# Two queues for one weight load: wq of problem A in two column ranges on the SP and ACT queues, x behind it on the ACT queue

## The chip, the cores and the metric

The kernel runs on one core of one Trainium2 chip. The metric is the device time of one execution in microseconds (us). Executions of one kernel agree within about 0.3%, so medians and ratios are quoted, and a trace is one execution and not the median one.

## The reference, cut to what matters

Two independent problems, A and B, of the same shape: one decode step of attention over the last 4096 positions of a key and value cache, 32 query heads on 16 key heads, batch 2, head size 128, model size 576.

```python
q = x @ wq                                   # (2, 576) @ (576, 4096), bf16
k = k_cache[:, :, -4096:, :]; v = v_cache[:, :, -4096:, :]
# cut: reshapes, and the repeat of each key and value head for its two query heads
scores = einsum("bhqd,bhkd->bhqk", q, k) * 128 ** -0.5
o = einsum("bhqk,bhkd->bhqd", softmax(scores), v)
out = o @ wo                                 # (2, 4096) @ (4096, 576)
# for A and for B; the outputs stand side by side
```

The bytes are almost all cache: 32 slabs of 4 MB (16 of K, 16 of V), beside 4.7 MB for each wq and each wo. x is 2.3 KB per problem.

## The kernel before

The cache slabs go through a ring of four SBUF slots (`NSLOT = 4`, 32 KB per partition and slot). At the start the two wq matrices lie in slots 0 to 2 of that ring. The first K slab goes to slot 3 at once; the second goes to slot 0 and must wait until q of A is done with wq of A. This ring of slots is one thing; where the text below speaks of a queue's ring, or of x's own ring, it means the row of packets that one queue (SP or ACT) has waiting on one DMA engine. A packet is one contiguous row of a copy, or the 4-byte write to a semaphore that ends a copy.

```python
def f_x(e):                                   # four copies of 2 rows of 1,152 bytes
    for P in range(NPROB):
        for h in range(2):
            last = e.dma_start(x8[4*P+2*h : 4*P+2*h+2, :], probs[P][0][:, 0, :]).then_inc(x_sem, 16)
    return last
x_dma = dma_op("act", x_sem, 2 * NPROB, f_x, [], "x")          # ACT queue, waits for nothing

for P in range(NPROB):                        # each wq: 128 rows of 36,864 bytes, SP queue
    def f_wq(e, P=P):
        src = probs[P][3].rearrange("a b -> (a b)").rearrange("(p f) -> p f", p=128)
        return e.dma_start(ringf[:, P*QW:(P+1)*QW], src).then_inc(wq_sem[P], 16)
    wq_dma[P] = dma_op("sp", wq_sem[P], 1, f_wq, [], "wq%d" % P)
# ... cut: x -> VectorE mask (xs8) -> TensorE transposes (xT) -> ACT copy (op_xev) ...
q_done[P] = pe(f_q, [wq_dma[P], op_xev], "q%d" % P)            # 36 matmuls for each P
# ... cut ...
stream = []                                   # order of the loads in the SP queue: K0 K1 K2 K3 V0 K4 V1 ...
for t in range(NSLAB + LAG):
    if t < NSLAB:
        stream.append(("K", t))
    if t >= LAG:
        i = t - LAG
        if i % 4 == 0 and i > 0:
            stream.append(("M", i // 4 - 1))  # a wo load
        stream.append(("V", i))
# ... cut ...
first_deps = {0: [q_done[0]], 1: [q_done[0], q_done[1]], 2: [q_done[1]], 3: []}   # by ring slot
```

Of the kernel before, what the change touches and what calls it, by code (L numbers as in the profile page):

```python
# [62 lines left out]
def build_kernel(nc, probs, out):  # L63
# [3 lines left out]
    NPROB = len(probs)  # L67
# [19 lines left out]
    UW = HD // 2  # L87
    NU = (2 * D) // 128
    QW = NU * UW
# [3 lines left out]
    with es:  # L93
# [50 lines left out]
        ringf = ring[:].rearrange("p r f -> p (r f)")  # L144
# [9 lines left out]
        sem = lambda name: es.enter_context(nc.semaphore(name))  # L154
# [3 lines left out]
        lastv_sem = [sem("lastv%d" % k) for k in range(2)]  # L158
        w_cuts = [0, 4, 7, 8]
        lastw_sem = [sem("lastw%d" % k) for k in range(2)]  # L160
        wq_sem = [sem("wq%d" % P) for P in range(NPROB)]
        wo_sem = [sem("wo%d" % r) for r in range(2)]
        x_sem = sem("xload")
        out_sem = sem("outdone")
# [4 lines left out]
        def dma_op(eng, sem_h, n_dmas, fn, deps, tag):  # L169
            op = S.add(eng, fn, deps, tag)  # L170
            dma_count[sem_h] = dma_count.get(sem_h, 0) + 16 * n_dmas
            op.dma = (sem_h, dma_count[sem_h])
            return op

        def f_x(e):
# [2 lines left out]
                for h in range(2):  # L178
                    last = e.dma_start(x8[4 * P + 2 * h:4 * P + 2 * h + 2, :], probs[P][0][:, 0, :]).then_inc(x_sem, 16)
            return last  # L180
        x_dma = dma_op("act", x_sem, 2 * NPROB, f_x, [], "x")

        wq_dma = {}
        for P in range(NPROB):
            def f_wq(e, P=P):
                src = probs[P][3].rearrange("a b -> (a b)").rearrange("(p f) -> p f", p=128)
                return e.dma_start(ringf[:, P * QW:(P + 1) * QW], src).then_inc(wq_sem[P], 16)
            wq_dma[P] = dma_op("sp", wq_sem[P], 1, f_wq, [], "wq%d" % P)

        pool = lambda fn, deps, tag: S.add("pool", fn, deps, tag)  # L190
        dve = lambda fn, deps, tag: S.add("dve", fn, deps, tag)
        act = lambda fn, deps, tag: S.add("act", fn, deps, tag)
        pe = lambda fn, deps, tag: S.add("pe", fn, deps, tag)
# [5 lines left out]
        p_ident_b = pool(lambda e: e.affine_select(ident_b[:], ones_b[:], [[-1, 128]], ALU.is_equal, 0.0,  # L199
                                                   base=0, channel_multiplier=1), [p_ones_b], "ident_b")  # L200
        p_zxU = pool(lambda e: e.memset(pTf[:, 0:XW].bitcast(FP32), 0.0), [], "zero_xU")

        def f_sel(e):
            last = None
            for p4 in range(4):
                b32, par = p4 // 2, p4 % 2
                last = e.affine_select(sel[:, p4, :].rearrange("d (a p) -> d a p", a=4),
                                       ones_b[:, :].rearrange("d (a p) -> d a p", a=4),
                                       [[0, 4], [-2, 32]], ALU.is_equal, 0.0, base=-(64 * b32 + par), channel_multiplier=1)
            return last  # L210
# [35 lines left out]
        def mm_held(e, o, wt, mv_, first, tile=None):  # L246
            size, at = tile or ((128, 128), (0, 0))
            return e.add_instruction(mybir.InstMatmult(  # L248
                name=nc.get_next_instruction_name(), engine=mybir.EngineType.PE,
                ins=[e.lower_ap(mv_), e.lower_ap(wt, for_matmul_weights=True)], outs=[e.lower_ap(o)],  # L250
                start_tensor_calc=first, stop_tensor_calc=True, bass_skip_group_check=True, ldweights=False,
                tile_size=size, tile_position=at))
# [14 lines left out]
        op_xev = act(f_xev, [op_xT, p_zxU], "xev")  # L267
        tb_consumer[n_] = op_xev

        q_done = {}  # L270
        QB = [OTB[0:32, :], PJT[0][0:32, :], PJT[1][0:32, :], STT[1][0:32, 512:1024]]
        for P in range(NPROB):
            def f_q(e, P=P):
                for u in range(NU):
                    for c in range(4):
                        wt, mv_ = xU[:, P, u, :], wqv[P][:, u, c * 512:(c + 1) * 512]
                        first = P == 0 and u == 0
                        if c == 0:
                            last = e.matmul(QB[c], wt, mv_, start=first, stop=True, skip_group_check=True)  # L279
                        else:  # L280
                            last = mm_held(e, QB[c], wt, mv_, first, ((128, 32), (0, 0)))
                return last
            q_done[P] = pe(f_q, [wq_dma[P], op_xev], "q%d" % P)
        q_ev = [act(lambda e, k=k: e.activation(qrow[32 * k:32 * k + 32, :], QB[k], ACTF.Copy), [q_done[1]], "qe%d" % k)
                for k in range(4)]

# [460 lines left out]
        for op in order:  # L747
            have = seen[op.eng]
            need = {}
            for d in op.deps:  # L750
# [3 lines left out]
                k = id(s_h)  # L754
# [30 lines left out]
def bass_concat_heads__sliding_block_cached__sliding_block_cached__decode_kernel(  # L785
    nc, A_x, A_k_cache, A_v_cache, A_wq, A_wo, B_x, B_k_cache, B_v_cache, B_wq, B_wo, out,
):
    build_kernel(nc, [(A_x, A_k_cache, A_v_cache, A_wq, A_wo), (B_x, B_k_cache, B_v_cache, B_wq, B_wo)], out)
# [28 lines left out]
```

## Time and profile before

| | before |
|---|---|
| median of 5 runs | 363.09 us (363.01 to 364.5) |
| bytes read | 153.1 MB; the SP queue's packets fill 98.5% of the span of the 16 engines |
| mean rate | 423 GB/s |
| x landed / first q matmul | 13.05 / 15.65 us |
| second K slab issued / its first packet | 25.75 / 34.08 us |

The first view is the page's row of 40 equal slices (9.07 us each): the busy share of the 16 DMA engines in tenths, and what they moved.

```profile
DMA  8999999999999999999999999999999999999995
GB/s 326 447 431 416 448 417 441 426 430 437 430 435 408 455 408 426 454 419 444 420 435 426 434 434 414 440 441 412 452 414 442 426 441 420 438 423 441 407 422 220
```

Only the first slice (start) and the last (tail) are below 400 GB/s. The engines never stand idle in between, so this kernel's time is its start, plus its bytes, plus its tail. Work on TensorE, VectorE or ACT matters only where it delays the release of a ring slot so long that the SP queue runs out of loads.

The next view is the sum by stretches of time; its columns are the stretch, its length, the busy time of each engine with the count of instructions, the granted TensorE clock, the DMA share, and GB/s.

```profile
core 0: us, PE busy (x) PEld busy (x) DVE busy (x) ACT busy (x) POOL busy (x), PEclk, DMA share, GB/s
34.00:40.00 6.00, 1.19 (x9) 0.58 (x9) 4.78 (x2) 2.99 (x10) 1.04 (x4) 0.76 1.01 437
40.00:100.00 60.00, 45.13 (x184) 9.37 (x110) 46.28 (x19) 4.98 (x8) 3.68 (x14) 0.85 1.01 434
```

The same six us from 34 to 40 in 40 slices of 0.15 us (busy share in tenths; slices so narrow show zeros even in a busy stretch):

```profile
DMA  5999550059995500599955005999550059995500
```

Then the start of the chain of waits (start, length, what), which shows that x, and not wq, lets q begin. wq of A, issued at 0.80, landed 13.8 us later, at 14.6.

```profile
1.94 11.11 DMA tmp<-in_B_x_dram
13.08 1.35 DVE pR L217
14.48 0.71 PE tb L258 x9
15.21 0.30 ACT pT L265 x2
15.65 0.59 PE ot L279
```

Last, the SP queue's own timeline around the second and third K slabs (start, length of the issue, queue, line, what):

```profile
25.75 0.54 SPq L377 DMA_DIRECT2D ring<-in_A_k_cache_dram  x1
33.52 1.18 SPq L377 DMA_DIRECT2D ring<-in_A_k_cache_dram  x2
```

The second K slab was issued at 25.75, when q of A was done. The packet records that lie in the trace (one for each packet: start, duration, size, queue) show the engines turning to it only at 34.08, when the first slab's rows had all been started.

### The profile page before, as it was taken

The page shows a single profiled execution, that of the slowest core. Times are in us where ns is not written, and L with a number is a line of the kernel's source. Part 1 is how long each engine was busy: PE and PEld are TensorE (multiplying, and loading weights), DVE is VectorE, ACT ScalarE, POOL GpSimd, SP SyncE. Part 2 cuts the span into 40 slices and gives each one's busy share as a digit, 9 for nine tenths or more (in the row PEclk, how much of TensorE's full clock was granted, in tenths as well). Part 3 has the DMA queues.
Part 4 walks back from the last instruction along what each step waited for, and adds up shares of the span by engine and source line. Part 5 has one row for each costly group of instructions (what it writes and reads, how often), then busy time and mean ns, then how long its engine had stood idle before and what let it go on. Part 6 is the DMA issues. An engine that isn't in the chain of part 4 may idle for free.

```text
span 362.7 us, 2629 instructions
## 1 busy us (share of the span) xinstructions
PE 237.2 (65%) x1295; PEld 58.2 (16%) x935; DVE 211.9 (58%) x141; ACT 46.2 (13%) x80; POOL 22.1 (6%) x83
## 2 busy tenths in 40 slices
PE   0397687767665868471696666562586677667666
PEld 0010111112111212020131211110112121112222
DVE  0201898495949392924919492942917658585522
ACT  1002100140041001300014001400005000500500
POOL 3100101100010001000010001000010001000000
PEclk9999698969898888986798989889789687889986
DMA  8999999999999999999999999999999999999995
GB/s 326 447 431 416 448 417 441 426 430 437 430 435 408 455 408 426 454 419 444 420 435 426 434 434 414 440 441 412 452 414 442 426 441 420 438 423 441 407 422 220
DMA packets 6228, 153.28 MB, mean 423 GB/s; under 512 B 700, under 2 KB 840, under 8 KB 1224
## 3 DMA queue, kind: packets, MB, share of 16 engines
q1 hardware_dynamic: 6196, 153.10, 98.5%
q8 instruction: 9, 0.15, 0.2%
q10 hardware_dynamic: 20, 0.01, 0.0%
q14 instruction: 3, 0.02, 0.0%
HBM read 153.10 MB, written 0.00 MB: 422 GB/s over the span
## 4 chain that ended last, share of the span: by engine, by line
DMA 48%; DVE 25%; PE 16%; issue 8%; ACT 1%; SPq 0%; POOL 0%; ACTq 0%
DMA ring<-in_B_k_cache_dram 25%; DVE xt L432 15%; DMA ring<-in_A_k_cache_dram 13%; DMA ring<-in_B_v_cache_dram 8%; PE st L248 5%; PE st L458 4%; DMA tmp<-in_B_x_dram 3%; PE pj L248 3%; DVE oR L564 2%; DVE mx L466 2%; DVE pT L505 2%; DVE tmp L557 2%; ACT pR L496 1%; PE ot L279 1%; PE pj L635 1%
## 5 line engine op out<-in xcount | busy, mean ns | idle before, releaser
L458 PE MATMUL st<-xt,zq 128*128 128x512 bf16 x256 | 122.6, 479 | 89.9 <-DVE xt L432 89.8
L432 DVE STREAM_TRANSPOSE xt<-ring 128x4096 f32<-128x4096 f32 x32 | 141.6, 4429 | 36.3 <-DMA ring<-in_A_k_cache_dram 20.8
L248 PE MATMUL st<-xt,zq 128*128 128x512 bf16 x256 | 121.2, 473 | 0.0
L496 ACT ACTIVATE pR<-st,bias 128x512 bf16<-128x512 f32 x32 | 40.0, 1415 | 217.7 <-DVE bias L489 217.7
L458 PEld LDWEIGHTS st<-xt,zq 128*128 128x128 bf16 x256 | 29.0, 113 | 212.7 <-DVE xt L432 106.7
L535 PE MATMUL ot<-ring,pT 128*32 128x512 bf16 x512 | 32.5, 395 | 6.9 <-DMA ring<-in_B_v_cache_dram 4.4
L489 DVE SCALAR_TENSOR_TENSOR bias<-vmask,tb,offm 128x4 f32<-128x4 f32 x8 | 1.8, 223 | 36.1 <-PE tb L486 36.1
L519 DVE TENSOR_REDUCE ssum<-tb 128x2 f32<-128x8 f32 x8 | 1.3, 162 | 36.0 <-PE tb L516 36.0
L505 DVE STREAM_TRANSPOSE pT<-pR 128x2048 bf16<-128x2048 bf16 x8 | 18.4, 2304 | 0.7 <-ACT pR L496 0.7
L424 POOL TENSOR_TENSOR zq<-qs,bmask 128x64 bf16<-128x64 bf16 x32 | 8.6, 292 | 165.7 <-PE st L248 143.8
L557 DVE SCALAR_TENSOR_TENSOR tmp<-ot,rsb,dmask 128x512 f32<-128x512 f32 x16 | 11.5, 719 | 8.5 <-PE ot L535 8.4
L535 PEld LDWEIGHTS ot<-ring,pT 128*32 128x32 bf16 x512 | 12.6, 99 | 22.0 <-DMA ring<-in_B_v_cache_dram 8.9
L564 DVE TENSOR_REDUCE oR<-tmp 128x128 f32<-128x512 f32 x15 | 15.6, 1042 | 0.5
L248 PE MATMUL pj<-ring,pT 128*32 128x512 bf16 x36 | 11.9, 417 | 0.0
L248 PE MATMUL pj<-wob,oM 128*2 128x288 bf16 x48 | 11.9, 286 | 0.0
L616 PE MATMUL pj<-wob,oM 128*2 128x288 bf16 x48 | 11.9, 286 | 0.0
L258 PE MATMUL tb<-ident_b,pR 8*128 8x8 bf16 x9 | 0.7, 198 | 14.5 <-DVE pR L217 14.5
L466 DVE TENSOR_REDUCE mx<-st 128x2 f32<-128x1024 f32 x8 | 9.7, 1214 | 0.1
L496 ACT ACTIVATION_READ_ACCUMULATOR pR<-st,bias 128x1 f32 x32 | 8.9, 278 | 0.0
L217 DVE TENSOR_TENSOR pR<-tmp,hmask 8x1152 bf16<-8x1152 bf16 x1 | 1.3, 1345 | 11.5 <-DMA tmp<-in_B_x_dram 11.5
L279 PE MATMUL ot<-ring,pT 128*32 128x512 bf16 x18 | 7.5, 419 | 0.5 <-ACT pT L265 0.5
L248 PE MATMUL st<-ring,pT 128*32 128x512 bf16 x18 | 7.3, 407 | 0.0
(69 smaller groups left out, 71.4 us busy)
## 6 DMA issues: line engine op xcount, KB each, us to landing
ring<-in_A_k_cache_dram SPq DMA_DIRECT2D x8, 4096.0 KB, 24.9
ring<-in_A_v_cache_dram SPq DMA_DIRECT2D x8, 4096.0 KB, 29.9
ring<-in_B_k_cache_dram SPq DMA_DIRECT2D x8, 4096.0 KB, 28.6
ring<-in_B_v_cache_dram SPq DMA_DIRECT2D x7, 4096.0 KB, 29.9
ring<-in_A_wq_dram SPq DMA_DIRECT2D x1, 4608.0 KB, 13.8
ring<-in_B_wq_dram SPq DMA_DIRECT2D x1, 4608.0 KB, 24.2
wob<-in_A_wo_dram SPq DMA_DIRECT2D x2, 2304.0 KB, 29.8
wob<-in_B_wo_dram SPq DMA_DIRECT2D x1, 2304.0 KB, 27.4
```

Source lines behind the costliest of these rows:

```text
L248: return e.add_instruction(mybir.InstMatmult(name=nc.get_next_instruction_name(), engine=mybir.EngineType.PE, ins=[e.lower_ap(mv_), e.lowe ...
L279: last = e.matmul(QB[c], wt, mv_, start=first, stop=True, skip_group_check=True)
L424: last = e.tensor_tensor(dst, src, msk, ALU.mult)
L432: Xop[(t, jh)] = dve(lambda e: e.transpose(xt[:, jh, :].bitcast(FP32).rearrange("p (kp x kt) -> p x kp kt", kp=2, kt=2), ring[:, r, jh * H ...
L458: last = e.matmul(ob, wt, mv_, start=first, stop=True, skip_group_check=True)
L466: ch[(G, "max")] = dve(lambda e: e.tensor_reduce(mx[:], st[:, :].rearrange("p (x t) -> p t x", t=2), AX.X, ALU.max), [Sop[(2 * G + 1, 1)]] ...
L496: last = e.activation(pR[:].rearrange("p (x k) -> p k x", k=4)[:, kv, :], st[:, :].rearrange("p (x t) -> p t x", t=2)[:, kv % 2, :], ACTF.Exp,
L505: pT_op[G] = dve(lambda e: e.transpose(pT[:, v, :].rearrange("p (w j q) -> p j w q", w=4, q=8), pR[:].rearrange("p (j w q) -> p j w q", w= ...
L535: last = e.matmul(OTB[32 * c:32 * c + 32, :], pT[:, v, base + 32 * c:base + 32 * c + 32], ring[:, r, jj * 128:(jj + 4) * 128], start=rd == ...
L557: evac_op[i] = dve(lambda e: e.scalar_tensor_tensor(tv, o, rsb[:, v, b:b + 1], dm, ALU.mult, ALU.mult), deps, "ev%d" % i)
L564: ch[(G, "red%d" % b)] = dve(lambda e: e.tensor_reduce(oR[:, b, :], tmp[:].rearrange("p (j d) -> p d j", j=4), AX.X, ALU.add), [evac_op[i] ...
L616: last = e.matmul(PJ[h], oM[:, j, :], mv_, start=start and j == 0, stop=True, skip_group_check=True)
```

## The change

The intent, as far as the edit tells it, is to have wq of A arrive by two queues at the same time, and to keep the small x copies from getting in the way of it: they now follow on the ACT queue, and also wait for a Pool memset.

```diff
-        wq_sem = [sem("wq%d" % P) for P in range(NPROB)]
+        wq_sem = [sem("wq%d" % P) for P in range(NPROB + 1)]
...
-        x_dma = dma_op("act", x_sem, 2 * NPROB, f_x, [], "x")
...
-            def f_wq(e, P=P):
-                src = probs[P][3].rearrange("a b -> (a b)").rearrange("(p f) -> p f", p=128)
-                return e.dma_start(ringf[:, P * QW:(P + 1) * QW], src).then_inc(wq_sem[P], 16)
-            wq_dma[P] = dma_op("sp", wq_sem[P], 1, f_wq, [], "wq%d" % P)
+            src = probs[P][3].rearrange("a b -> (a b)").rearrange("(p f) -> p f", p=128)
+            cuts = [("sp", 0, 5 * UW), ("act", 5 * UW, QW)] if P == 0 else [("sp", 0, QW)]
+            wq_dma[P] = []
+            for k, (q, c0, c1) in enumerate(cuts):
+                def f_wq(e, P=P, src=src, c0=c0, c1=c1, k=k):
+                    return e.dma_start(ringf[:, P * QW + c0:P * QW + c1], src[:, c0:c1]).then_inc(wq_sem[2 * k + P], 16)
+                wq_dma[P].append(dma_op(q, wq_sem[2 * k + P], 1, f_wq, [], "wq%d_%d" % (P, k)))
...
         p_zxU = pool(lambda e: e.memset(pTf[:, 0:XW].bitcast(FP32), 0.0), [], "zero_xU")
+        x_dma = dma_op("act", x_sem, 2 * NPROB, f_x, [p_zxU], "x")
...
-            q_done[P] = pe(f_q, [wq_dma[P], op_xev], "q%d" % P)
+            q_done[P] = pe(f_q, wq_dma[P] + [op_xev], "q%d" % P)
```

UW is 2,048 columns and QW is 9 UW, so each of the 128 rows of 36,864 bytes becomes one of 20,480 bytes on SP and one of 16,384 bytes on ACT.

## The prediction

> What bounds the kernel. The page puts the DMA share at 9 tenths in 38 of 40 slices, mean 423 GB/s for 153.28 MB; the first slice (326 GB/s) is the start, the last (220) the tail. The SP queue carries 98.5%. The trace's packet records show every engine starting a 36,864-byte wq row each 1.36 us and a 32 KB cache row each 1.21 us, without a gap from 2.1 to about 354 us. So the time is start + bytes + tail; compute matters only where it lets the SP queue run dry.
>
> What moves. Before, four x copies (1,152-byte rows, two engines) sit on the ACT queue from 0.8 us and land at 13.05 (the chain of waits: 11.11 us). The Trainium skill, "DMA: Bandwidth & Descriptors", section "Queues, rings and completion order", says that an engine round-robins between queue rows packet by packet. The packet records agree: each x copy is a data and a semaphore packet per engine, and after the first copy those start 1.36 to 1.45 us apart, one per wq row. x, not wq, lets q start: wq A lands at 14.6, and x + 1.35 (VectorE) + 0.7 (TensorE) + 0.3 (ACT) gives 15.5; the first q matmul is at 15.65.
>
> After, the same bytes of wq A run on two rings: a 20 KB and a 16 KB packet, together one old row, so wq A still lands at about 14.5. The same page, section "Issuing engines are not separate DMA queues", says both issuers share the same engines; only under 0.5 us of issue time could be gained. But x now stands in the ACT ring behind eight 16 KB packets, is reached at about 14 us, and then its eight packets alternate with the eight rows of wq B. I estimate from the 1.36 us row that x lands at 24 to 25.2 us. The wait for the Pool memset (done by 2.2 us) costs nothing.
>
> What follows. q of A starts at 26.5 to 27.8 instead of 15.65, takes about 10 us as before, and is done at 36.6 to 37.9 instead of 25.7. The second K slab waits for it (ring slot 0). Before, it was issued 7 to 8 us early: the last row of the first slab started at 33.2, the next at 34.4. Now it is late; with 1.3 us from issue to first packet (0.80 to 2.12 at the start) its first row starts at 37.9 to 39.2: a hole of 3.5 to 4.8 us in the DMA, plus up to 0.8 for refilling (the first row at the start cost 2.13, not 1.36). The third slab waits for q of B, done at 44.5 to 46, while the second arrives until about 48: no second hole. Scores start 10 to 11 us later, but slots were released 8 to 20 us ahead of need (fifth K slab 54.4 against about 73), so this is absorbed; the tightest, the sixth (issued 83.3, needed about 92), keeps some 3 us. All of the hole is on the critical path; the tail is unchanged.
>
> Sum: 363.1 + 4.3 = 367.4 us (+1.2%). Range 364.6 to 369.8. Faster by over 2%: 0.02; within: 0.90; slower: 0.08.
>
> To check: VectorE's idle time for x near 22 to 23 us instead of 11.5; first q matmul near 27; low bandwidth at 35 to 39 us; DMA otherwise full; tail as before.
>
> What would make it wrong: x's packets not alternating with wq B (x lands near 15: time unchanged); a later slot release falling behind, opening a second hole (over 370); two rings filling the start better (0.5 us faster).

## The result, and the profile after

| | before | after |
|---|---|---|
| median of 5 runs | 363.09 us | 369.11 us (367.95 to 369.92) |
| ratio | | 1.0157, 95% interval 1.0133 to 1.0181 |
| x landed / first q matmul | 13.05 / 15.65 | 25.16 / 27.75 us |
| second K slab issued / first packet | 25.75 / 34.08 | 37.16 / 38.51 us |

Ratios here are the mean time of one kernel's runs over the mean of the other's runs of the same rounds, so they are not quite the ratio of the medians. The change costs 1.6%, 5.7 us. The same slices of the page, now 9.18 us each:

```profile
DMA  8996899999999999999999999999999999999996
GB/s 314 458 425 289 343 411 445 439 418 450 407 453 409 450 432 420 434 441 414 447 411 441 432 432 425 437 425 446 414 443 413 447 428 432 427 432 432 416 415 253
```

Two slices, the fourth and the fifth, fell to 289 and 343 GB/s; everything after them is as full as before. The stretches of the same cuts:

```profile
34.00:40.00 6.00, 6.00 (x30) 0.68 (x7) 4.72 (x2) 0.00 (x0) 0.00 (x0) 1.00 0.28 87
40.00:100.00 60.00, 42.93 (x195) 9.02 (x113) 37.42 (x14) 8.46 (x18) 4.35 (x16) 0.89 1.01 433
```

A finer cut of 34 to 40 us, into 40 slices of 0.15 us, shows where the engines stood (busy share in tenths). Slices so narrow show a few zeros in a busy stretch too, because the view does not spread a packet over all of its time: what counts is the unbroken run of 30 zeros, 34.0 to 38.5 us, in which no packet starts. The rows started before it (the last at 33.60) end between 34.0 and 34.8 us, and each engine's next row starts between 38.5 and 39.2: each stood idle for some 4.4 to 4.8 us.

```profile
DMA  0000000000000000000000000000009909900000
```

From 34 to 40 us the engines moved 87 GB/s instead of 437, while TensorE was busy for all 6.00 us. The chain of waits and the SP queue say why:

```profile
3.44 21.72 DMA tmp<-in_B_x_dram
25.18 1.36 DVE pR L220
26.59 0.71 PE tb L261 x9
27.32 0.30 ACT pT L268 x2
27.75 0.59 PE ot L282
37.16 0.54 SPq L380 DMA_DIRECT2D ring<-in_A_k_cache_dram  x1
```

x took 21.72 us to land where it took 11.11. The steps behind it have the same lengths as before (1.36, 0.71, 0.30), so q of A starts 12.1 us later. It takes 0.7 us less than in before's trace (experiment 9), and the second K slab is issued at 37.16, 11.4 us later. The slack was 34.08 - 25.75 - 1.34 = 7.0 us (issue to first packet took 1.3 us in later runs where the queue was empty), so 4.4 us are left as the hole: 38.51 against 34.08.

The packet records show x's way through the ring. These are the starts of x's packets on one of the two engines that carry it (each of the four copies is one data packet of 1,152 bytes and one semaphore packet), in us:

| | copy 1 | copy 2 | copy 3 | copy 4 |
|---|---|---|---|---|
| before: data, semaphore | 1.72, 2.19 | 5.31, 6.72 | 8.08, 9.49 | 10.86, 12.26 |
| after: data, semaphore | 14.81, 16.22 | 17.58, 18.99 | 20.36, 21.76 | 23.13, 24.54 |

Two things delay it in after. Its first packet comes 13.1 us later, because eight rows of wq and their semaphore write stand ahead of it in its own ring, and each of those has its turn only after a packet of the other ring. The semaphore write counts: on this engine it came at 13.44, the first row of wq of B ran from 13.45 to 14.81, and only then was it x's turn. Then its eight packets take 9.7 us more, one for each 1.36 us row of wq of B. That two rows of x use two engines is what the Trainium skill, "DMA: Bandwidth & Descriptors", section "Why a DMA increments its semaphore by 16 and not by 1", says of a copy with two rows; the records agree with eight data packets for four copies, that is two for each.

A caution on the two traces. The profiled run of before had a time of 363.97, 0.9 above its median, and its last load packet ended 3.4 us before the end of the span; in after that tail was 2.6 us. So the spans (362.7 and 367.1) differ by 4.4 us only, but the last load packets (359.29 and 364.54) by 5.25. What makes the tail differ is said under "The sum over the runs".

### The profile page after: what moved, and what is told of

Read it like the earlier page. It is cut to its first block, busy times and chain, and to the rows that moved or that the text cites. A ratio compares the mean times of both kernels' runs of the same rounds, so it can differ in the third digit from the quotient of the medians. Undisturbed runs are those within 1.5% of the kernel's fastest.

```text
span 367.1 us, 2627 instructions
## 1 busy us (share of the span) xinstructions
PE 235.5 (64%) x1294; PEld 57.5 (16%) x935; DVE 211.4 (58%) x141; ACT 46.4 (13%) x80; POOL 22.2 (6%) x83
## 4 chain that ended last, share of the span: by engine, by line
DMA 35%; DVE 32%; PE 21%; issue 8%; ACT 2%; POOL 1%; ACTq 0%; SPq 0%; DVEq 0%; POOLq 0%
DVE xt L435 20%; DMA ring<-in_B_k_cache_dram 16%; DMA ring<-in_B_v_cache_dram 8%; PE st L251 7%; DMA tmp<-in_B_x_dram 6%; PE st L461 6%; DMA wob<-in_B_wo_dram 5%; PE pj L251 4%; DVE oR L567 3%; DVE pT L508 2%; DVE mx L469 2%; DVE tmp L560 2%; PE pj L619 2%; ACT pR L499 1%; PE ot L282 1%
## 5 line engine op out<-in xcount | busy, mean ns | idle before, releaser
L538 PE MATMUL ot<-ring,pT 128*32 128x512 bf16 x512 | 33.6, 405 | 4.5 <-DVE ssum L522 2.5
L220 DVE TENSOR_TENSOR pR<-tmp,hmask 8x1152 bf16<-8x1152 bf16 x1 | 1.3, 1347 | 23.6 <-DMA tmp<-in_B_x_dram 23.6
L282 PE MATMUL ot<-ring,pT 128*32 128x512 bf16 x18 | 7.3, 405 | 0.5 <-ACT pT L268 0.5
## 6 DMA issues: line engine op xcount, KB each, us to landing
wob<-in_A_wo_dram SPq DMA_DIRECT2D x2, 2304.0 KB, 27.8
ring<-in_A_wq_dram SPq DMA_DIRECT2D x1, 2560.0 KB, 13.8
```

Of the source, the lines that this page charges most:

```text
L282: last = e.matmul(QB[c], wt, mv_, start=first, stop=True, skip_group_check=True)
L538: last = e.matmul(OTB[32 * c:32 * c + 32, :], pT[:, v, base + 32 * c:base + 32 * c + 32], ring[:, r, jj * 128:(jj + 4) * 128], start=rd == ...
```

## The experiments

Eleven kernels ran; all gave correct results. The theory: x lands late because of its place in the ACT ring and because rings take turns packet by packet; that makes q of A late, the second K slab late, and the DMA engines idle; this hole is the whole loss. The rivals: (R1) cutting wq over two rings costs in itself; (R2) scores that start 10 us late push later slot releases; (R3) rings share by bytes and not by turns; (R4) the wait for the Pool memset is a part of it. Each set of runs has its own runs of before on the same chip; their medians were 363.36 (experiments 1, 2, 5 and 6), 363.18 (3, 4, 7 and the first run of 8) and 363.37 (the second run of 8, 9 and 10).

### 1. Late x without the split (against R1)

```diff
 # in the kernel before
-        x_dma = dma_op("act", x_sem, 2 * NPROB, f_x, [], "x")
...
             wq_dma[P] = dma_op("sp", wq_sem[P], 1, f_wq, [], "wq%d" % P)
+        x_dma = dma_op("sp", x_sem, 2 * NPROB, f_x, [], "x")
```

> The kernel before, wq of A in one piece on SP; the x copies are moved to the SP queue behind wq of B. Theory (late x alone makes the loss): x lands at 24 to 25.5 us, the first q matmul at about 27.5, the second K slab's first packet at 38 to 38.5, bandwidth falls to nothing from about 35 to 38, time 368.3 to 369.5, as after. Rival (cutting wq of A over two rings costs in itself): nothing is cut here, so the loss should be clearly smaller than after's 6 us.

Measured: 369.49 us, ratio 1.0171 (1.0156 to 1.0186). Its timeline has x consumed at 25.49 and the second K slab issued at 38.34:

```profile
25.49 1.34 DVE L217 TENSOR_TENSOR pR<-tmp,hmask 8x1152 bf16<-8x1152 bf16 x1 [23.93 <-DMA tmp<-in_B_x_dram]
38.34 0.53 SPq L377 DMA_DIRECT2D ring<-in_A_k_cache_dram  x1
```

Nothing is cut here, nothing runs on two rings, and the loss is the same. A late x is enough. (The first packet of the second slab came at 39.67, past the 38.5 that I had expected: q of A began at 28.06 and not at 27.5, and it took 10.25 us; on its length see experiment 9.)

### 2. Fill the hole (against R2)

```diff
 # in the kernel after
             if t < NSLAB:
                 stream.append(("K", t))
+            if t == 0:
+                stream.append(("M", 0))
...
-                if i % 4 == 0 and i > 0:
+                if i % 4 == 0 and i > 4:
```

> The kernel after with one edit: the first wo load (2.36 MB, no dependency) moves in the SP queue from among the V slabs to just behind the first K slab. Theory (all of the loss is the DMA engines standing idle before the second K slab): x still lands at about 25, q of A still starts at 27.75, but the wo load takes 5.4 us of engine time where the hole was, so the time returns to 362.7 to 363.7. Rival (scores that start 10 us late push later slot releases, or the split itself costs): x and q are as late as in after, so the time stays near 369.

Measured: 363.93 us, ratio to before 1.0009 (0.9992 to 1.0026). x and q are as late as in after (first q matmul 27.69, second K slab issued at 38.07), but 34 to 40 us are full:

```profile
34.00:40.00 6.00, 6.00 (x29) 0.68 (x7) 4.97 (x2) 0.00 (x0) 0.00 (x0) 1.00 1.02 425
```

Against after's 87 GB/s in the same stretch this is the decisive line: with the lateness untouched and only the idle engine time used for bytes that had to be moved anyway, the loss is gone within what this run resolves (its median lies 0.2 us above the range I had written). The 10 us by which the scores start late cost nothing that can be measured.

### 3. Control: the early wo load in the kernel before

The same edit as in 2, made in before.

> Control for the filling run: the kernel before with the first wo load just behind the first K slab. Theory: the DMA engines are busy there anyway, the same bytes in another order: 362.8 to 363.6. If the early wo load were a gain by itself, it would be below 361.

Measured: 363.42 us, ratio 1.0004 (0.9984 to 1.0023). The early wo load is no gain by itself; in 2 it only filled the hole.

### 4. The split with x behind wq of A on SP (R1 again)

```diff
 # in the kernel after
-        x_dma = dma_op("act", x_sem, 2 * NPROB, f_x, [p_zxU], "x")
...
                 wq_dma[P].append(dma_op(q, wq_sem[2 * k + P], 1, f_wq, [], "wq%d_%d" % (P, k)))
+            if P == 0:
+                x_dma = dma_op("sp", x_sem, 2 * NPROB, f_x, [], "x")
```

> The kernel after, wq A still on two rings, but the x copies go to the SP queue between wq A and wq B. Theory: x is still behind wq A but no longer alternates with wq B; it lands at 13.6 to 14.6, q of A starts at 16 to 17.2, the second K slab is issued 6 us early, no hole: 362.8 to 363.4. Rival (cutting wq A over two rings costs in itself): still above 365.

Measured: 363.34 us, ratio 1.0003 (0.9985 to 1.0022). x's packets started at 13.62 to 13.81, VectorE took x up at 15.00, some 0.4 us later than expected, and q of A began at 17.57. The split is in, and nothing is lost. R1 has now failed from both sides.

### 5. The cut moved to 8 to 1 (turns or bytes, R3)

```diff
 # in the kernel after
-            cuts = [("sp", 0, 5 * UW), ("act", 5 * UW, QW)] if P == 0 else [("sp", 0, QW)]
+            cuts = [("sp", 0, 8 * UW), ("act", 8 * UW, QW)] if P == 0 else [("sp", 0, QW)]
```

> The kernel after with wq A cut 8 to 1 instead of 5 to 4: ACT's packets are 4 KB, 0.5 MB in all. Theory (turns go by packet): still eight pairs of packets before x's turn, so x lands at 24 to 25.5 as after and the time is 368.3 to 369.7. Rival (turns go by bytes, or x waits only for the bytes ahead of it in its ring): x's turn comes after about 1 MB, it lands before 13 us, and the time is 363.

Measured: 369.02 us, ratio 1.0153 (1.0129 to 1.0177). ACT's share of wq is down from 2.1 to 0.5 MB, and x's first packet starts at 14.74 where it started at 14.81; VectorE takes x up at 24.99 where it was 25.18:

```profile
24.99 1.35 DVE L220 TENSOR_TENSOR pR<-tmp,hmask 8x1152 bf16<-8x1152 bf16 x1 [23.43 <-DMA tmp<-in_B_x_dram]
```

What stands ahead of x counts in packets, not in bytes: eight rows of 4 KB held it as long as eight of 16 KB. The Trainium skill says the rule ("DMA: Bandwidth & Descriptors", section "Queues, rings and completion order": each engine round-robins between the rows it has work for, a whole packet at a time); this pair of runs shows it.

### 6. x ahead of wq's second part on the ACT queue

```diff
 # in the kernel after
+        x_dma = dma_op("act", x_sem, 2 * NPROB, f_x, [], "x")      # now above the wq loads
...
-        x_dma = dma_op("act", x_sem, 2 * NPROB, f_x, [p_zxU], "x")
```

> The kernel after, but the x copies stand in the ACT queue ahead of wq A's second part and wait for nothing. Theory (rings alternate packet by packet, whatever the size): x lands at about 8 us, but on the two engines that carry x its small packets use up the turns, so most of wq A's second part alternates with the 36 KB rows of wq B and lands only at 22.5 to 24.5; q of A starts at about 24.4, the second K slab at about 35.4, a hole of 1.2 to 1.7 us plus 0.7 refill: 364.7 to 365.7. Rival (only x's place behind wq counts): x is first, so q starts at about 15 and the time is 363.

Measured: 366.47 us, ratio 1.0090 (1.0074 to 1.0105). The obvious repair is only half of one. The chain of waits of this run, whose first long wait is for wq and not for x any more:

```profile
2.24 22.92 DMA ring<-in_A_wq_dram
25.16 0.09 issue
25.25 0.58 PE ot L282
```

VectorE had x at 9.38, but q of A waited until 25.16 for the second part of wq: on the two engines that carry x, its eight small packets used up eight turns, and the 16 KB packets behind them had to alternate with the 36 KB rows of wq of B. The mechanism is as expected; the time was 0.8 us above the range (up to 365.7). The second part landed at 25.16 and not by 24.5, but that does not explain it: q of A then took 9.6 us, and the second K slab was issued at 34.87, before the 35.4 that I had expected. By the packets the second slab is 2.5 us late in this trace, which is little more than the hole expected; the tail of the trace is 0.7 us longer than after's (see the sum over the runs).

### 7. x later, but inside the slack

```diff
 # in the kernel before: wq of B in two parts on SP, x between them (cut: f_wq takes its columns, one semaphore more)
-        x_dma = dma_op("act", x_sem, 2 * NPROB, f_x, [], "x")
...
-            wq_dma[P] = dma_op("sp", wq_sem[P], 1, f_wq, [], "wq%d" % P)
+            for k, (c0, c1) in enumerate([(0, QW)] if P == 0 else [(0, 4 * UW), (4 * UW, QW)]):
+                if k == 1:
+                    x_dma = dma_op("sp", x_sem, 2 * NPROB, f_x, [], "x")
+                wq_dma[P].append(dma_op("sp", wq_sem[P + k], 1, ...))
```

> The kernel before, with wq of B cut 4 to 5 on SP and the x copies between its two parts. Theory (lateness of x is free until the second K slab's issue falls behind the queue): x lands at 18.5 to 20, 6 us later than before, q of A is done at about 31, first packet of the second K slab ready before 34: no hole, 362.9 to 363.5. Rival (each us of late x costs, through the late scores): 365 to 366.

Measured: 364.02 us, ratio 1.0017 (1.0001 to 1.0034). VectorE took x up at 19.60, 6.5 us later than in before, and the second K slab was issued at 31.79, 6.0 us later; its first packet started at 33.93, no later than in before. The issue, which in before's trace stood at 25.75:

```profile
31.79 0.54 SPq L380 DMA_DIRECT2D ring<-in_A_k_cache_dram  x1
```

So 6 us of lateness cost about 0.6 us, where 12 us cost 5.7: there is a threshold, and a cost for each us (which would have made 2 to 3 us here) is refuted. The median is 0.5 us above the range that I had written, and where the 0.6 us go stays open: the last load packet of its trace ended at 359.97, against 359.27 to 359.46 in before and in experiments 4, 8 (before with the wait) and 10. This run sits within a us of the threshold, so that a slower q of A (experiment 9) would already open a small hole; that is argued and not shown, for its profile shows none.

### 8. The wait for the Pool memset, alone (R4)

```diff
 # in the kernel before
-        x_dma = dma_op("act", x_sem, 2 * NPROB, f_x, [], "x")
...                                     # after the memset p_zxU
+        x_dma = dma_op("act", x_sem, 2 * NPROB, f_x, [p_zxU], "x")
```

> The kernel before plus the wait of the x copies for the Pool memset, nothing else. Theory: x is issued at 2.2 instead of 0.8, every one of its packets then waits a 36 KB row, and it lands at 14 to 16 us; q of A starts 1 to 3 us later, inside the slack: 362.9 to 363.5. Rival (the wait is a part of the loss): over 364.

Measured: 363.67 us, ratio 1.0013 (0.9985 to 1.0041). x was taken up at 15.60, 2.5 us later than in before, and the time did not move by more than the scatter (its four runs span 363.14 to 365.13).

The other way round, after without the wait:

```diff
 # in the kernel after
-        x_dma = dma_op("act", x_sem, 2 * NPROB, f_x, [p_zxU], "x")
+        x_dma = dma_op("act", x_sem, 2 * NPROB, f_x, [], "x")
```

> The kernel after without the wait of the x copies for the Pool memset. Theory: x is issued at 1.2 instead of 2.2 but its packets stand behind the same eight packets in the ring, so it lands at 24.3 to 25.5 all the same: 368 to 370. Rival (the wait is a part of the loss): 1 us less or more.

Measured: 369.07 us, ratio 1.0155 (1.0136 to 1.0174); x taken up at 25.22. R4 has failed too: behind the packets of wq it does not matter when x is issued.

### 9. TensorE warm before q of A (a scatter that the prediction missed)

The prediction's sum was 4.3 us and the loss 5.7. In the profiles of the runs with a late x, q of A took from 9.4 to 10.5 us. This edit keeps TensorE busy with matmuls of no use until x arrives; they write a score bank that the first score matmul overwrites.

```diff
 # in the kernel after, ahead of the transposes of x
+        def f_warm(e):
+            o, mv_ = STT[0][:, 0:512], zq[:].rearrange("d p m w -> d (p m w)")[:, 0:512]
+            last = e.matmul(o, ones_b[:, :], mv_, start=True, stop=True, skip_group_check=True)
+            for _ in range(89):
+                last = mm_held(e, o, ones_b[:, :], mv_, True)
+            return last
+        pe(f_warm, [p_zq, p_ones_b], "warm")
```

> The kernel after plus 90 matmuls of no use on TensorE from about 4 to 26 us, so that its clock is up when q of A starts. Theory (the length of the hole is x's lateness plus the length of q of A, and the slow first rows of q are the part of it that varies): x lands at 25.2 as before, q of A takes 7.8 to 8.2 us instead of 9.4 to 10.5, the second K slab's first packet comes at 36.9 to 37.4, the hole is 2.9 to 3.4 us plus 0.7: 366.2 to 367.2, and its runs lie within 1 us of each other. Rival (the 1.4 us by which after exceeds the prediction come from later slots or the tail): still about 369 with the same scatter.

Measured: 367.2 us (five runs, 366.74 to 367.67), ratio 1.0099 (1.0083 to 1.0114). x is taken up at 25.32, as late as ever. q of A took 7.93 us, its second K slab came at 35.86 with the first packet at 37.18, and the runs lie within 0.93 us of each other, those of after within 1.97 (five runs each, so the spreads alone prove little). The reason is TensorE's pace at the start of q, seen in the counts of matmuls in stretches of 2 us. First after:

```profile
28.00:30.00 2.00, 2.00 (x6) 1.00 1.10 475
30.00:32.00 2.00, 2.00 (x9) 1.00 1.06 459
32.00:34.00 2.00, 2.00 (x11) 1.00 0.76 328
```

then after without the wait (experiment 8), a run with the same code for TensorE:

```profile
28.00:30.00 2.00, 2.00 (x6) 1.00 1.18 508
30.00:32.00 2.00, 2.00 (x6) 1.00 1.02 442
32.00:34.00 2.00, 2.00 (x9) 1.00 0.80 344
```

and the warmed kernel:

```profile
28.00:30.00 2.00, 2.00 (x10) 1.00 1.21 524
30.00:32.00 2.00, 2.00 (x11) 1.00 0.95 410
32.00:34.00 2.00, 2.00 (x11) 1.00 0.87 377
```

Six matmuls in 2 us is about half the later pace of eleven (their starts are 0.43 us apart, and then 0.22). In the first two views the 1.00 in the column of the granted clock says nothing: the view counts time without a clock record as full clock, and the first record comes only when the slow pace ends. How long the slow pace lasts differs from run to run: the last slow matmul started at 30.27 in after's trace and at 32.44 in the second, though q began at 27.75 and 27.80. The Trainium skill, "TensorE: Matmul & The Clock Gate", section "What's actually happening", explains it by a window of about 3.4 us that runs free of the kernel, after which a busy TensorE gets its full clock. The traces agree: the first clock record, of full clock, comes at 30.72 in after and at 32.70 in the second, where the pace changes, and all later records of a trace stand whole multiples of 3.41 us apart. In before the same scatter is there (q of A took 10.07 us in its trace and 10.84 in the control of experiment 3), but the 7 us of slack swallow it.

### 10. A version that might beat both: x first on the SP queue

```diff
 # in the kernel after
+        x_dma = dma_op("sp", x_sem, 2 * NPROB, f_x, [], "x")       # now above the wq loads
...
-        x_dma = dma_op("act", x_sem, 2 * NPROB, f_x, [p_zxU], "x")
```

> A version that might beat both: wq A on two rings as in after, x copies at the head of the SP queue. Theory: wq A's second part on ACT keeps the engines busy from the start, x is through its ring by about 8 us at the latest, q of A starts when wq A is in, at 14 to 14.6 instead of 15.65; but the time hangs on the DMA engines, which were never idle before, so no gain: 362.7 to 363.6. If an early q were worth anything by itself: below 362.

Measured: 363.14 us (five runs, 363.09 to 363.28), ratio 0.9989 (0.9977 to 1.0002). q of A begins at 14.40, 1.25 us earlier than in before, and the split does no harm. But an earlier q is worth nothing where the engines were never idle: this version is not told apart from before, and no version beat it.

### The sum over the runs

The loss can be read from the packet records alone, as the delay of the second K slab's third round of rows against before (36.50 us), and set beside the measured loss (ratio minus one, times 363.2 us):

| kernel | second slab issued | its first packet | third round late by | measured loss |
|---|---|---|---|---|
| after | 37.16 | 38.51 | 5.1 us | 5.7 us |
| late x, no split (1) | 38.34 | 39.67 | 5.8 | 6.2 |
| cut 8 to 1 (5) | 38.07 | 39.41 | 5.6 | 5.6 |
| after without the wait (8) | 38.16 | 39.49 | 5.8 | 5.6 |
| warm TensorE (9) | 35.86 | 37.18 | 3.8 | 3.6 |
| x ahead on ACT (6) | 34.87 | 36.20 | 2.5 | 3.3 |

Each row is one profiled run against a mean of several, so agreement within 0.8 us is what can be asked for.

A part of that scatter has nothing to do with the change. The tail, from the last load packet to the end of the span, took 2.54 to 2.59 us in seven of the thirteen traces (after's is one), and in these the clock records show TensorE at full clock in it. In the other six (before and experiments 1, 2, 5, 6 and 9) it took 3.09 to 3.55 us, and in each of them a record of half clock reaches into the tail, whose work on TensorE took 1.61 us in before against 0.65 in after. So up to 1 us of a run's time hangs on how the clock happens to stand at its end, in before as much as in after.

## Why the prediction was right

The forecast was 367.4 us (364.6 to 369.8); measured 369.11, inside the range. Point by point:

- "The time is start + bytes + tail", and the hole is all of the loss: right. Filling the hole alone brought 363.93.
- "x lands at 24 to 25.2 us": right, 25.16, by the stated path: behind eight rows, then alternating with wq of B. Experiments 5 and 6 show that it is turns that count. It was one turn more than forecast: the semaphore write of wq's second part stands in the ring too, so x was reached at 14.81 and not at "about 14", and 25.16 is the top of the range.
- "No bandwidth is gained" by a second queue (the Trainium skill, "DMA: Bandwidth & Descriptors", section "Issuing engines are not separate DMA queues"): right. The first row of wq of B started at 13.40 us where it had started at 13.51; the part of wq of A on SP landed 13.8 us after its issue, as the whole did before, and the last packet of the part on ACT ended at 14.24.
- First q matmul at 26.5 to 27.8: 27.75. A hole from 35 to 39 us, no second one, later slot releases absorbed: right, as the slices and experiment 2 show. "The tail is unchanged" holds only to within the 1 us by which tails differ whatever the kernel.
- "Takes about 10 us as before, and is done at 36.6 to 37.9": the five profiles with a late x (after, experiments 1, 2 and 5, and after without the wait) gave 9.4 to 10.5 us, 10.2 on average, and ends at 37.1 to 38.3. The length was about right; the ends are late because q began at 27.56 to 28.06, near or above the top of the forecast. What I did not see is that the scatter of TensorE's slow start, hidden by slack in before, would now go straight into the time. The warmed kernel took 2.1 us off the loss by removing the slow start; most of that was in the forecast's 10 us, so it is not the size of the forecast's error. That after's own trace has its first packet at 38.51, in the middle of the forecast 37.9 to 39.2, is luck: its q was the shortest of the five, and made up for x's extra turn.
- A slip: my packet times were counted from a zero 0.31 us too early. "33.2" and "34.4" should be 32.9 and 34.1, the start of packets 1.8 and not 2.1, so 0.80 to first packet was 1.0 us. This made the hole 0.3 us too short. The issue-to-first-packet time of 1.3 us that I took from it was, by luck, what later runs had (1.32 to 1.35).
- The refill of up to 0.8 us: in after the second round of rows came 1.92 us behind the first instead of 1.21, so 0.7; in experiment 1 it came 1.44 us behind, so only 0.2.

Together: with the first packet at 38.5 to 39.7 instead of 34.1 the hole is 4.4 to 5.6 us, and with the refill the third round of rows is 5.1 to 5.8 us late; I had 4.3. The range of the forecast was wide enough for this, and 369.11 lies near its top (one of the five runs, 369.92, lies above it). The other forecast to check, VectorE's wait for x, was 23.6 us where 22 to 23 had been said.

## What to carry to other kernels

A small copy issued on the queue of a large load waits for turns and not for bytes: count the packets ahead of it in its own ring, semaphore writes included, and the size of the packets in the other ring that come between them. In a kernel that is bound by DMA, an input that arrives late costs nothing until the slack of the next load that depends on it is used up, and then it costs one for one; so measure that slack (issue to first packet) before moving a load. And a late dependency can be made harmless by moving a load without dependencies into the hole.

## What the Trainium skill lacked or had wrong

- "DMA: Bandwidth & Descriptors", section "Queues, rings and completion order", counts a turn as a packet of some 9 to 17 descriptors, but does not say what that is for plain row copies. In these traces a contiguous row was one turn whether it had 4 KB or 36 KB (0.5 and 2.1 MB ahead of x gave 14.74 and 14.81 us), and the 4-byte semaphore write of a copy took a turn of its own: four copies of one row per engine took eight turns, 9.7 us beside 36 KB rows.
- The same page does not spell out that the second queue's turns are lost to whatever stands first in it: with x first on the ACT ring, the 16 KB packets behind it landed at 25.16 us instead of about 14.
- The same page, section "Specifications", gives 0.6 us to the first byte for the SP and ACT queues. Counted from the end of the issue it was 0.6 us at the start of the kernel (0.80 + 0.39 to 1.82) and 0.8 us in the hole (37.16 + 0.54 to 38.51). What decides the size of a hole is longer, and no page has it: 1.32 to 1.35 us from the start of the issue, and then 0.2 (experiment 1) to 0.7 us (after) until rows followed at their usual distance.
- "TensorE: Matmul & The Clock Gate", section "What's actually happening", puts the scatter of the warm-up at 500 ns either way and says not to count on a fixed number of slow matmuls. Here the last slow matmul moved by 2.2 us between two runs whose q began within 0.05 us of each other, and q of A took 9.4 to 10.5 us with a late x, against 7.93 us warm. The 500 ns are too few; the advice holds.
